# Interleaved row blocks in the last unit's gate product, one store for each of its row tiles, and pair 5's query sums and key copies at the end of the step

## Chip, cores and metric

The kernel runs on one core of a Trainium2 chip. The metric is the device time of one execution in microseconds; the time given for a kernel is the median of its runs. The engines are named as in the profile: PE is TensorE, ACT is ScalarE, DVE is VectorE, POOL is GpSimd, SP is SyncE.

## The reference

Attention with pooled queries, and after it a feed-forward part with a gate:

```python
q_pool = q.reshape(B, H, S // 2, 2, D).mean(axis=3)      # B=8, H=8, S=1152, D=64
scores = (1 / sqrt(D)) * q_pool @ k.transpose(0, 1, 3, 2)
attn = softmax(scores)                                   # over 1152 keys
x = (attn @ v).transpose(0, 2, 1, 3).reshape(B * 576, 512)
out = ((x @ w1) * (x @ w2) @ w3) @ w_out                 # d_ff = 1024, out 4608 x 512 float32
```

## The kernel before

**Pairs and steps.** Two heads make a pair; there are 32 pairs, with 576 pooled queries and 9 blocks of 128 keys each. The scores of all pairs, laid end to end, are cut into 324 chunks of 512 columns. The main loop (`for it in range(NIT)`, L598) has 108 steps. A step issues three chunks: `scores` (L301) makes the matmuls into one of three PSUM buffers named `psc`, which are taken in turn, and `expo` (L319) takes the exponential on ScalarE into a ring in SBUF. After the chunks a step issues attention matmuls (`attend`, L330, whose counts are written out by hand in `PVS`), and between them one or two groups from a queue (`group`, L551): a group of kind "F" has a PSUM buffer `ff` of its own, a group of kind "X" takes the next `psc` buffer. A group issues its matmuls and then its eviction. Each engine works through its instructions in the order in which the program issues them.

**What the groups are.** First the weights: w3 is transposed (`w3_group`, L402, evicted to `w3T` at L411) and multiplied by w_out (`T_group`, L414, evicted to `T16` at L422), so that w3 @ w_out becomes one matrix. Then the feed-forward units: 512 rows of x each, nine in all (`ffn_groups`, L425). A unit has 8 pairs of groups `pa` and `pb` (x @ w1 and x @ w2, transposed: features on partitions, rows in columns), whose product is written to `gT` at L446, and then four row blocks of 128 rows (`rows`, L449), which multiply `gT` by `T16`, evict to a row tile `osb` (L461 on ScalarE, L464 on VectorE) and store it (L473). The first seven units are issued between the attention's groups; what remains runs behind the attention, with `tail` set.

**Preparing a pair.** Pairs 1 to 7 are prepared on VectorE and TensorE. `prep_stage` (L162) issues two VectorE instructions: the sums of neighbouring queries (L121, from the staged queries `qst`) and a copy of the keys into another order (L165, from `kst`). One step later `prep_groups` (L270) is put at the head of the queue: TensorE transposes sums and keys (L278, L169), and VectorE copies them to `qT` and `kT` (L284 to L292). From pair 8 on, `prep_dma` does this with GpSimd and DMA transposes instead. The loop calls `prep_stage` in two places:

```python
        if 5 <= staged < NPE and it >= first_it(staged) - 3:     # L615: ahead of the step's groups
            prep_stage(staged)
            staged += 1
...
        if staged < 5 and it >= first_it(staged) - 2:            # L648: behind the step's groups
            prep_stage(staged)
            staged += 1
            more_loads(staged)
```

`first_it(5)` is 16, so pair 5 is prepared in step 13, whose chunks are 39 to 41. That step's groups are a w3 transposition (kind F) and a T group (kind X). Loads of queries, keys and values are issued on POOL's queue, in a written order.

**Stores.** Row p * 9 + c of a batch's output belongs to query block c, so a row tile of 128 rows covers two query blocks of 64 rows, the lower and the upper half of its partitions. Each half is stored by a DMA of its own, 64 rows with a step of 9 rows in the output. The very last row block (`final`) is computed in pieces of 256, 128 and 128 columns, each evicted and stored by itself; there the upper half's store is issued on ScalarE's queue, all others on SyncE's.

Of the kernel before, what the change touches and what calls it, by code (L numbers as in the profile page):

```python
# [14 lines left out]
SQ = 576  # L15
NJ = 9
# [7 lines left out]
def kernel(  # L24
# [11 lines left out]
    nc = tc.nc  # L36
    B, H, S, D = q.shape
    dm = H * D
# [6 lines left out]
    NPE = 8  # L45
# [13 lines left out]
    T16 = const.tile([128, NF, dm], FP16)  # L59
# [39 lines left out]
    def load(P):  # L99
        if P < NP:  # L100
            load_k(P)
            load_q(P)
            load_v(P)
# [32 lines left out]
    def prep_dma(P):  # L136

        pool_q(P, 2)
        for p in (P, P + 1):
            new_kq(p)  # L140
            nc.gpsimd.tensor_copy(  # L141
                out=new_kc(p).rearrange("p j u d -> p u j d").bitcast(mybir.dt.int32),
                in_=kst.pop(p).bitcast(mybir.dt.int32))
        for p in (P, P + 1):
            nc.sync.dma_start_transpose(
                out=kT[p], in_=kcs[p].rearrange("p j u d -> p (j u d)"))
            if p == P:
                nc.sync.dma_start_transpose(
                    out=qTs[P // 2], in_=qps[P // 2].rearrange("p c u d -> p (c u d)"))
# [12 lines left out]
    def prep_stage(P):  # L162

        pool_q(P)
        nc.vector.tensor_copy(out=new_kc(P).rearrange("p j u d -> p u j d"), in_=kst.pop(P))  # L165
# [135 lines left out]
    def scores(c):  # L301
        t = psum.tile([128, 2, CH], FP32, tag="psc", bufs=3, name="psc")
        psc[c] = t
        if 3 <= c < 10:
            nc.tensor.matmul(t[:, 0], ones[:, 0:128], ones, start=True, stop=True)
        g = c * CH
        while g < (c + 1) * CH:
            J = g // SQ
            P, j = divmod(J, NJ)
            f0 = g - J * SQ  # L310
            ln = min(SQ - f0, (c + 1) * CH - g)
            o = g - c * CH
            for u in range(2):
                s = slice(64 * u, 64 * u + 64)
                nc.tensor.matmul(t[:, u, o:o + ln].rearrange("p (c f) -> p c f", f=64), kT[P][s, j, :],  # L315
                                 qT[P][s, f0 // 64:(f0 + ln) // 64], start=True, stop=True)
            g += ln

    def expo(c):  # L319
        r = (c * CH) % RING  # L320
        g = (c - RING // CH + 1) * CH
        if g > 0:
            Pg, Jg = divmod((g - 1) // SQ, NJ)
            assert nb >= 90 * Pg + 45 + 5 * Jg + 5
        nc.scalar.activation(out=er[:, :, r:r + CH], in_=psc.pop(c), func=AF.Exp,  # L325
                             bias=0.0, scale=SCALE)
# [69 lines left out]
    tail = False  # L396
# [28 lines left out]
    def ffn_groups(t):  # L425
        t0 = 512 * t
        gT = ffp.tile([128, NF, 512], FP16, tag="g", name="gT")
        asb = {}

        def half(ft, name):  # L430
            w = w1sb if name == "pa" else w2sb

            def mm(p, mc):
                nc.tensor.matmul(p, w[:, mc, ft * 128:ft * 128 + 128],  # L434
                                 xT[:, mc, t0:t0 + 512],
                                 start=(mc == 0), stop=(mc == NC - 1))

            def end(p):
                if name == "pa":
                    asb[ft] = ffp.tile([128, 512], FP32, tag="asb", name="asb")  # L440
                    if tail:
                        nc.scalar.copy(out=asb[ft], in_=p)  # L442
                    else:
                        nc.vector.tensor_copy(out=asb[ft], in_=p)  # L444
                else:
                    nc.vector.tensor_mul(out=gT[:, ft, :], in0=p, in1=asb.pop(ft))  # L446
            return name, FP32, NC, mm, end

        def rows(i, o, n):  # L449

            def mm(p, ft):
                nc.tensor.matmul(p[:, 0:n], gT[:, ft, 128 * i:128 * i + 128],  # L452
                                 T16[:, ft, o:o + n],
                                 start=(ft == 0), stop=(ft == NF - 1))

            def end(p):
                if o == 0:
                    osbs[i] = ffp.tile([128, dm], FP32, tag="osb", bufs=6, name="osb")
                osb = osbs[i][:, o:o + n]
                if tail and not (final and o):  # L460
                    nc.scalar.activation(out=osb, in_=p[:, 0:n], func=AF.Copy, bias=0.0,  # L461
                                         scale=1.0 / (SCL * SCL))
                else:
                    nc.vector.tensor_scalar_mul(out=osb, in0=p[:, 0:n],  # L464
                                                scalar1=1.0 / (SCL * SCL))
                if not final and o + n < dm:
                    return
                cs = slice(o, o + n) if final else slice(0, dm)
                for z in range(2):
                    b, f = divmod(t0 + 128 * i + 64 * z, SQ)  # L470
                    dst = out[b * SQ:(b + 1) * SQ, :].rearrange("(p c) m -> c p m", c=NJ)
                    eng = nc.scalar if final and z else nc.sync
                    eng.dma_start(out=dst[f // 64][:, cs], in_=osbs[i][64 * z:64 * z + 64, cs])  # L473
            final = t == n_units - 1 and i == 3
            return "pp", FP32, NF, mm, end

        osbs = {}
        for ft in range(NF):
            yield half(ft, "pa")
            yield half(ft, "pb")  # L480
        for i in range(4):
            last = t == n_units - 1 and i == 3
            widths = (256, 128, 128) if last else (512,) if tail else (256, 256)
            for x, n in enumerate(widths):
                yield rows(i, sum(widths[0:x]), n)


    NCHUNK = NP * PAIR // CH
# [6 lines left out]
        out=ident, in_=ident, compare_op=ALU.not_equal, fill=1.0,  # L495
# [16 lines left out]
    loaded, staged, prepped, copied = 8, 1, 1, 1  # L512
# [24 lines left out]
    n_units = NT // 512  # L537
# [37 lines left out]
    def first_it(P):  # L575
        return P * PAIR // (CH * BURST)
# [21 lines left out]
    for it in range(NIT):  # L598
        at = it * BURST * CH / PAIR
        while early and it >= early[0][0]:  # L600
            queue.append(early.pop(0)[1])
        while next_unit < EARLY:
            last_b = (512 * (next_unit + 1) - 1) // SQ
            if it < 3 or reached[it - 2] < 360 * (last_b + 1):
                break
            gens.append(ffn_groups(next_unit))
            next_unit += 1
        for w in range(BURST):
            if it == 0 and w == 2:
                some()  # L610
            if it == 1 and w == 1:
                rest()
            scores(BURST * it + w)
            expo(BURST * it + w)
        if 5 <= staged < NPE and it >= first_it(staged) - 3:  # L615
            prep_stage(staged)
            staged += 1
        while 8 <= loaded < NPE + 2 and at >= loaded - 3.4:
            load(loaded)
            loaded += 1  # L620
        urgent = False
        if prepped < NPE:
            if it >= first_it(prepped) - (1 if prepped < 5 else 2):
                queue[0:0] = prep_groups(prepped)
                prepped += 1
                urgent = True
        elif prepped < NP and at >= prepped - 1.95:
            prep_dma(prepped)
            if loaded < NP:
                settled(prepped)  # L630
                load_two(loaded)
                loaded += 2
            prepped += 2
        if NPE <= copied < NP and at >= copied - 1.1:
            copy_v(copied)
            copied += 1
        n = PVS[it]
        left = 45 - nb % 45
        brief = bool(queue) and queue[0][2] == 1
        a = left if left < n else 8 if brief and it > 8 and 8 < n < 40 and 8 < left < 45 else 0  # L640
        assert nb + n <= NPV and ready(nb + n - 1, BURST * it)
        pv(a)
        if head():
            group("F")
        if head() and (n < 40 or urgent or it < 17):
            group("X")
        pv(n - a)
        if staged < 5 and it >= first_it(staged) - 2:  # L648
            prep_stage(staged)
            staged += 1  # L650
            more_loads(staged)
        if copied < NPE and at >= copied + (0.25 if copied < 5 else 0):
            copy_v(copied)
            copied += 1
        reached.append(nb)
# [6 lines left out]
    tail = True  # L662
# [36 lines left out]
```

The softmax here doesn't subtract the row's maximum and nothing guards it: scores larger than these inputs give would overflow.

## Time and profile before

| | |
|---|---|
| median of 13 runs | 419.07 us (418.31 to 421.5) |
| the profiled execution | 418.76 us, of which its span 417.0 us |
| mean granted TensorE clock | 0.997 |
| ScalarE's exponentials (L325) | 324, 307.3 us busy, 1028 ns each |
| attention matmuls (L340) | 2880, 110.3 us busy |
| gate products (L446) | 72, 49.8 us busy, 691 ns each |
| output stores (L473) | 76 DMAs |

The span runs from the first to the last instruction of the program. A line of a timeline gives the start, the length, the engine, the source line, the operation with its tiles and shapes, the number of instructions merged, and in brackets how long the engine had been idle before and what ended that. An engine's name with a q behind it (SPq, ACTq) is its instruction queue issuing a DMA. A line of waits gives the engine and line that waited, what it waited for, the total, the number of times and the longest. "To landing" is the time from a DMA's issue until its completion was signalled.

### The profile page before, as it was taken

What the parts mean: (1) busy time and instruction counts of PE and PEld (TensorE: products, weight loads), DVE (VectorE), ACT (ScalarE), POOL (GpSimd) and SP (SyncE); (2) the same over time, 40 slices, a digit from 0 to 9 for tenths busy, and PEclk for the clock granted to TensorE, in tenths of its full rate; (3) what the DMA queues carried; (4) which work ended last, traced back from release to release, by engine and by line L of the source; (5) the groups of instructions that cost most, each with busy time, mean ns of one, the idle gap of its engine ahead of it and who ended that gap; (6) DMA issues with size and microseconds to landing.
All of it is one profiled execution on the core that took longest, in us unless ns stands there. A gap on an engine that the chain in (4) does not pass through costs nothing.

```text
span 417.0 us, 12724 instructions
## 1 busy us (share of the span) xinstructions
PE 406.1 (97%) x5497; PEld 270.4 (65%) x5497; DVE 199.7 (48%) x408; ACT 326.0 (78%) x356; POOL 121.2 (29%) x161
## 2 busy tenths in 40 slices
PE   8999899999999999999999999999999999999994
PEld 5677777766775677666866686668656866544442
DVE  3546666455445643544455644554555345613130
ACT  5999899889888899988888898898888999032321
POOL 7533431343435262534524305252430000000000
PEclk9999999999999999999999999999999999999998
DMA  8999999799999999999999959997993351050404
GB/s 202 202 204 189 184 205 191 117 158 157 146 168 204 158 187 191 171 166 146 189 216 139 182 92 200 146 176 137 193 165 63 53 80 31 2 116 2 101 0 103
DMA packets 96489, 59.76 MB, mean 143 GB/s; under 512 B 65584, under 2 KB 86704, under 8 KB 96432
## 3 DMA queue, kind: packets, MB, share of 16 engines
q0 software_dynamic: 26928, 32.97, 50.5%
q1 hardware_dynamic: 69264, 25.84, 37.3%
q8 instruction: 43, 0.70, 0.7%
q10 hardware_dynamic: 240, 0.13, 0.1%
q14 instruction: 14, 0.11, 0.1%
HBM read 67.11 MB, written 9.44 MB: 184 GB/s over the span
## 4 chain that ended last, share of the span: by engine, by line
PE 85%; DMA 10%; ACT 2%; POOL 1%; issue 1%; DVE 1%; ACTq 0%; POOLq 0%
PE po L340 19%; PE psc L315 17%; PE pa L434 16%; PE pp L452 16%; PE pb L434 15%; DMA qst<-in_q_dram 4%; DMA kst<-in_k_dram 3%; DMA w3h<-in_moe_w_dram 2%; ACT er L325 2%; PE pT L418 2%; DMA er<-in_k_dram 1%; POOL kst L88 0%; POOL w3h L379 0%; PE t L169 0%; POOL vst L95 0%
## 5 line engine op out<-in xcount | busy, mean ns | idle before, releaser
L325 ACT ACTIVATE er<-psc 128x1024 f16<-128x1024 f32 x324 | 307.3, 1028 | 41.4 <-PE psc L315 41.2
L340 PEld LDWEIGHTS <-er 128*128 128x128 f16 x2880 | 103.3, 97 | 22.0 <-issue 5.9
L340 PE MATMUL po<-vt,er 128*128 128x65 f16 x2880 | 110.3, 193 | 0.0
L315 PE MATMUL psc<-qT,kT 64*128 64x512 f16 (+7 forms) x1152 | 95.0, 285 | 3.5 <-ACT er L325 2.0
L446 DVE TENSOR_TENSOR gT<-pb,asb 128x512 f16<-128x512 f32 x72 | 49.8, 691 | 56.0 <-PE pb L434 55.2
L434 PE MATMUL pa<-xT,w1sb 128*128 128x512 f16 x288 | 74.2, 380 | 0.0
L434 PE MATMUL pb<-xT,w2sb 128*128 128x512 f16 x288 | 74.1, 380 | 0.0
L452 PE MATMUL pp<-T,gT 128*128 128x256 f16 (+2 forms) x496 | 67.9, 290 | 0.0
L315 PEld LDWEIGHTS <-kT 64*128 64x128 f16 x1152 | 45.5, 94 | 28.5 <-issue 9.8
L452 PEld LDWEIGHTS <-gT 128*128 128x128 f16 x496 | 45.9, 98 | 18.4 <-issue 3.7
L444 DVE COPY asb<-pa 128x512 f32<-128x512 f32 x56 | 38.7, 691 | 38.2 <-PE pa L434 37.1
L434 PEld LDWEIGHTS <-w2sb 128*128 128x128 f16 x288 | 26.4, 98 | 32.7 <-issue 3.9
L434 PEld LDWEIGHTS <-w1sb 128*128 128x128 f16 x288 | 25.1, 98 | 30.1 <-issue 6.2
L121 POOL TENSOR_TENSOR qp<-qst 128x1152 f16<-128x1152 f16 x12 | 28.3, 2355 | 55.9 <-issue 27.6
L464 DVE TENSOR_SCALAR osb<-pp 128x256 f32<-128x256 f32 (+1 forms) x50 | 21.0, 419 | 38.6 <-PE pp L452 38.6
L353 DVE RECIPROCAL rz<-po 128x5 f32<-128x5 f32 x64 | 12.4, 193 | 47.9 <-PE po L340 47.5
L141 POOL COPY kc<-kst 128x576 int32<-128x576 int32 x24 | 16.5, 688 | 57.0 <-issue 41.7
L357 DVE TENSOR_TENSOR xn<-po,rz 128x320 f16<-128x320 f32 x64 | 31.5, 492 | 2.2
L95 POOL DMA_DIRECT2D vst<-in_v_dram x32 | 23.4, 742 | 11.9 <-DVE T L422 4.3
L461 ACT ACTIVATE osb<-pp 128x512 f32<-128x512 f32 (+1 forms) x12 | 7.0, 579 | 24.0 <-PE pp L452 20.4
L88 POOL DMA_DIRECT2D kst<-in_k_dram x31 | 22.6, 745 | 9.3 <-DVE kT L285 2.3
L442 ACT COPY asb<-pa 128x512 f32<-128x512 f32 x16 | 9.4, 586 | 16.5 <-PE pa L434 16.5
(49 smaller groups left out, 151.9 us busy)
## 6 DMA issues: line engine op xcount, KB each, us to landing
vst<-in_v_dram POOLq DMA_DIRECT2D x32, 288.0 KB, 10.4
out_dram<-osb SPq DMA_DIRECT2D x70, 128.0 KB, 2.5
qst<-in_q_dram POOLq DMA_DIRECT2D x31, 288.0 KB, 7.2
kst<-in_k_dram POOLq DMA_DIRECT2D x31, 288.0 KB, 12.8
w3h<-in_moe_w_dram POOLq DMA_DIRECT2D x3, 512.0 KB, 14.3
xT<-in_moe_w_out_dram POOLq DMA_DIRECT2D x4, 256.0 KB, 10.1
w1sb<-in_moe_w_dram POOLq DMA_DIRECT2D x2, 512.0 KB, 16.8
w2sb<-in_moe_w_dram POOLq DMA_DIRECT2D x2, 512.0 KB, 16.9
```

Of the source, the lines that this page charges most:

```text
L88: nc.gpsimd.dma_start(out=kst[P].rearrange("p u j d -> p u (j d)"), in_=k[b, h0:h0 + 2].rearrange("u (p j) d -> p u (j d)", j=NJ))
L95: nc.gpsimd.dma_start(out=vst[P].rearrange("p u j d -> p u (j d)"), in_=v[b, h0:h0 + 2].rearrange("u (p j) d -> p u (j d)", j=NJ))
L121: eng.tensor_tensor(out=qps[pp][r].rearrange("p c u d -> p u c d"), in0=src[:, :, :, 0, :], in1=src[:, :, :, 1, :], op=ALU.add)
L315: nc.tensor.matmul(t[:, u, o:o + ln].rearrange("p (c f) -> p c f", f=64), kT[P][s, j, :], qT[P][s, f0 // 64:(f0 + ln) // 64], start=True, ...
L325: nc.scalar.activation(out=er[:, :, r:r + CH], in_=psc.pop(c), func=AF.Exp, bias=0.0, scale=SCALE)
L340: nc.tensor.matmul(po[P, u][:, VW * x:VW * x + D + 1], er[:, u, r:r + 128], vts[P % 4][:, u, j, 0:D + 1], start=(m == 0), stop=(m == 44), ...
L357: nc.vector.tensor_tensor(out=xn[:, P % 2, :, u, :], in0=acc[:, :, 0:D], in1=rz.to_broadcast([128, 5, D]), op=ALU.mult)
L434: nc.tensor.matmul(p, w[:, mc, ft * 128:ft * 128 + 128], xT[:, mc, t0:t0 + 512], start=(mc == 0), stop=(mc == NC - 1))
L444: nc.vector.tensor_copy(out=asb[ft], in_=p)
L446: nc.vector.tensor_mul(out=gT[:, ft, :], in0=p, in1=asb.pop(ft))
L452: nc.tensor.matmul(p[:, 0:n], gT[:, ft, 128 * i:128 * i + 128], T16[:, ft, o:o + n], start=(ft == 0), stop=(ft == NF - 1))
L464: nc.vector.tensor_scalar_mul(out=osb, in0=p[:, 0:n], scalar1=1.0 / (SCL * SCL))
```

## The change

Two parts, independent of each other.

In the last unit (`t == n_units - 1`) the gate product is written with the two halves of each 128-row block interleaved: column r of the lower half and column r of the upper half stand side by side. A row tile's partitions then hold rows of the two query blocks in turn, and in the output such a pair of rows is 1024 contiguous elements. One DMA on SyncE's queue stores the row tile. The last row block is computed in two pieces of 256 columns, the first evicted by ScalarE and the second by VectorE, each stored by one DMA on SyncE's queue. For all other units evictions and stores stay as they are.

Pair 5's `prep_stage` moves from the first of the two places in the loop to the second, in the same step 13; pairs 6 and 7 stay in the first. `more_loads`, which is called behind it there, issues loads only when its argument is 2, 3 or 4.

```diff
                 else:
-                    nc.vector.tensor_mul(out=gT[:, ft, :], in0=p, in1=asb.pop(ft))
+                    o, a = gT[:, ft, :], asb.pop(ft)
+                    if t == n_units - 1:
+                        o = o.rearrange("f (i r z) -> f i z r", i=4, z=2)
+                        p = p.rearrange("f (i z r) -> f i z r", i=4, z=2)
+                        a = a.rearrange("f (i z r) -> f i z r", i=4, z=2)
+                    nc.vector.tensor_mul(out=o, in0=p, in1=a)
...
-        def rows(i, o, n):
+        def rows(i, s, n):
...
-                cs = slice(o, o + n) if final else slice(0, dm)
+                cs = slice(n * s, n * s + n) if final else slice(0, dm)
+                if t == n_units - 1:
+                    b, f = divmod(t0 + 128 * i, SQ)
+                    dst = out[b * SQ:(b + 1) * SQ, :].rearrange("(p c) m -> p c m", c=NJ)
+                    nc.sync.dma_start(out=dst[:, f // 64:f // 64 + 2, cs], in_=osbs[i][:, cs])
+                    return
                 for z in range(2):
                     b, f = divmod(t0 + 128 * i + 64 * z, SQ)
                     dst = out[b * SQ:(b + 1) * SQ, :].rearrange("(p c) m -> c p m", c=NJ)
-                    eng = nc.scalar if final and z else nc.sync
-                    eng.dma_start(out=dst[f // 64][:, cs], in_=osbs[i][64 * z:64 * z + 64, cs])
+                    nc.sync.dma_start(out=dst[f // 64], in_=osbs[i][64 * z:64 * z + 64])
...
-            last = t == n_units - 1 and i == 3
-            widths = (256, 128, 128) if last else (512,) if tail else (256, 256)
-            for x, n in enumerate(widths):
-                yield rows(i, sum(widths[0:x]), n)
+            if tail and not (t == n_units - 1 and i == 3):
+                yield rows(i, 0, 512)
+            else:
+                yield rows(i, 0, 256)
+                yield rows(i, 1, 256)
...
-        if 5 <= staged < NPE and it >= first_it(staged) - 3:
+        if 6 <= staged < NPE and it >= first_it(staged) - 3:
...
-        if staged < 5 and it >= first_it(staged) - 2:
+        if staged < 6 and it >= first_it(staged) - (2 if staged < 5 else 3):
             prep_stage(staged)
             staged += 1
             more_loads(staged)
```

More of the change, by code (lines that the diff above doesn't have):

```diff
@@ L445, in end @@
                 else:
-                    nc.vector.tensor_mul(out=gT[:, ft, :], in0=p, in1=asb.pop(ft))
+                    o, a = gT[:, ft, :], asb.pop(ft)
[4 more added lines that the diff above has]
+                    nc.vector.tensor_mul(out=o, in0=p, in1=a)
             return name, FP32, NC, mm, end
-        def rows(i, o, n):
+        def rows(i, s, n):
             def mm(p, ft):
                 nc.tensor.matmul(p[:, 0:n], gT[:, ft, 128 * i:128 * i + 128],
-                                 T16[:, ft, o:o + n],
+                                 T16[:, ft, n * s:n * s + n],
                                  start=(ft == 0), stop=(ft == NF - 1))
             def end(p):
-                if o == 0:
+                if s == 0:
                     osbs[i] = ffp.tile([128, dm], FP32, tag="osb", bufs=6, name="osb")
-                osb = osbs[i][:, o:o + n]
-                if tail and not (final and o):
+                osb = osbs[i][:, n * s:n * s + n]
+                if tail and not (final and s):
                     nc.scalar.activation(out=osb, in_=p[:, 0:n], func=AF.Copy, bias=0.0,
@@ L465, in end @@
                                                 scalar1=1.0 / (SCL * SCL))
-                if not final and o + n < dm:
+                if not final and n * (s + 1) < dm:
                     return
-                cs = slice(o, o + n) if final else slice(0, dm)
+                cs = slice(n * s, n * s + n) if final else slice(0, dm)
[4 more added lines that the diff above has]
+                    return
                 for z in range(2):
```

## The prediction

> **What bounds the kernel now.** I read the page's engine rows first, then the waits of TensorE, then the timelines round the one wait that the moved step could touch, and last the tail after the final matmul.
>
> ```profile
> PE 406.1 (97%) x5497; PEld 270.4 (65%) x5497; DVE 199.7 (48%) x408; ACT 326.0 (78%) x356; POOL 121.2 (29%) x161
> PE 85%; DMA 10%; ACT 2%; POOL 1%; issue 1%; DVE 1%; ACTq 0%; POOLq 0%
> ```
>
> TensorE (PE) is busy 97% of the 417.0 us, and the chain that ended last is 85% TensorE. So time can be won only where TensorE stands still, or before its first and after its last matmul. Its waits (engine, line, releaser: total us, times, longest):
>
> ```profile
> PE psc L315 <- ACT er L325: 2.0, 7, 0.5
> PE psc L315 <- DVE T L422: 0.9, 1, 0.9
> ```
>
> One wait is on VectorE (DVE), a single time, 0.9 us. From 73 us on, TensorE has no recorded wait above 0.06 us: what it is late at 73 us, it is late at the end. VectorE and TensorE round that wait (start, length):
>
> ```profile
> 46.26 0.76 DVE L121 TENSOR_TENSOR qp<-qst 64x1152 f16<-64x1152 f16 x1 [1.68 <-DMA qst<-in_q_dram]
> 47.05 0.46 DVE L165 COPY kc<-kst 128x1152 f16<-128x1152 f16 x1
> 47.43 0.68 DVE L411 COPY w3T<-w3t 128x1024 f16<-128x1024 f16 x1
> 48.03 0.42 DVE L422 CAST T<-pT 128x256 f16<-128x256 f32 x1
> ```
>
> ```profile
> 45.36 1.04 PE L418 MATMUL pT<-xT,w3T 128*128 128x256 f16 x8
> 46.23 0.83 PE L340 MATMUL po<-vt,er 128*128 128x65 f16 x22
> 46.99 0.61 PE L315 MATMUL psc<-qT,kT 64*128 64x384 f16 x8
> 48.50 0.39 PE L315 MATMUL psc<-qT,kT 64*128 64x512 f16 x2 [0.89 <-DVE T L422]
> ```
>
> This is pair 5's preparation (step 13). VectorE stood 1.68 us before its query sums because pair 5's queries landed only at 46.24. Two evictions, ready in PSUM since 45.52 (L406) and 46.40 (L418), queued behind it and ran at 47.43 and 48.03. Scores take one of three `psc` buffers in turn; chunk 44 needed the one the late T eviction held, so TensorE stood 0.89 us. ScalarE (ACT) felt it one chunk later, idle 0.75 us:
>
> ```profile
> 51.09 1.02 ACT L325 ACTIVATE er<-psc 128x1024 f16<-128x1024 f32 x1 [0.75 <-PE psc L315]
> ```
>
> The tail:
>
> ```profile
> 411.11 1.73 ACTq L473 DMA_DIRECT2D out_dram<-osb  x1
> ```
>
> ```profile
> 411.59 0.29 DVE L464 TENSOR_SCALAR osb<-pp 128x128 f32<-128x128 f32 x1 [0.15 <-PE pp L452]
> ```
>
> ```profile
> 413.59 0.81 ACTq L473 DMA_DIRECT2D out_dram<-osb  x1
> ```
>
> ```profile
> out_dram<-osb ACTq DMA_DIRECT2D x1, 32.0 KB, 2.1
> ```
>
> The last matmul ends at 411.57 and the last eviction at 411.89, but the last store is issued only at 413.59: ScalarE's queue has three stores, the first took 1.73 us to issue, the second started at 412.94. The last lands at 413.59 + 2.12 = 415.70. SyncE then runs through its closing waits to 416.15, and the closing barrier ends the span at 417.0.
>
> **What the Trainium skill says.** "VectorE: DVE Perf Modes", section "Why PSUM operands drop a tier": an fp32 operand in PSUM holds the operation at 1x. The gate product is already there (512 elements in 691 ns, 0.74 elements per ns, overhead included), so a spread output has no faster mode to lose. "DMA: Bandwidth & Descriptors", section "Issuing engines are not separate DMA queues": stores from two engines share the same 16 DMA engines and a second issuer saves only issue time; here ScalarE's issues took 0.55 to 1.73 us and SyncE's 0.47 to 0.60, so it did not even save that. Same page, "Why a DMA increments its semaphore by 16 and not by 1": a transfer uses the largest count up to 16 that divides the slowest dimension of both sides. The new store has 64 rows on one side and 128 partitions on the other, so 16; no run here shows this shape yet.
>
> **The change, part by part.**
>
> 1. *Gate products of the last unit* (8 of 72, L446): same 512 elements, only the fp16 output steps by two. No row shows a stepped output. Bounds: 0.69 us each (no change) to twice, 1.38; a gain is excluded, since the work is the same. VectorE is idle 1.03 us before each (0.69 in a period of 1.73 us), so even 1.38 is hidden, and the last product, begun at 404.72, is needed by the first row block's eighth matmul at about 404.61 + 7 x 0.216 = 406.1. I take 0; if the cover were gone, up to 0.1.
>
> 2. *Row tiles 0 to 2 of the last unit*: one 256 KB store for two of 128 KB. Before, the pair was issued within 1.11 us (406.995 to 408.10) and TensorE needs 1.73 us per tile. No effect on the end except for what is still moving when the last tile comes.
>
> 3. *Row tile 3*: 256 + 128 + 128 columns become 256 + 256. TensorE: the 16 matmuls of 128 columns start 0.056 us apart, 0.90 us; 8 of 256 at 0.109 are 0.87 us: -0.02. Its last eviction is 128x256 on VectorE, 0.42 us (the other L464 rows) instead of 0.29. So: matmuls end 411.55, VectorE ends 411.99, SyncE issues at 412.01 (it issued 0.03 us after the eviction for tile 0). SyncE is free: tile 2's single store goes out at 410.45, tile 3's first half, evicted at 411.08, at 411.11. The six stores of the last tile become two, all of ScalarE's disappear.
>
> Landing: a 128 KB store took 2.24 to 2.39 us from issue, so 414.25 to 414.40 if nothing is in front. In front are tile 2's 256 KB and tile 3's first 128 KB. The first tile's 256 KB moved from 408.17 to 409.35 (about 0.6 us per 128 KB, first byte 1.2 us after issue, 0.5 us from last byte to landing). So tile 2's data run 411.65 to 412.85, the first half's to 413.45, the last half's to 414.05, landing 414.55. I take 414.5, a gain of 1.2 us on 415.70. SyncE's closing waits are about 0.06 us each and six of them followed the last landing; with another store last in the round of eight semaphores, 0 to 6 follow: +0.1 on average. **Tail: 1.3 us**, bounds 0.9 (256 KB issue as slow as 0.6 us, more contention) and 1.7.
>
> 4. *Pair 5's preparation to the end of step 13.* It is two VectorE instructions and issues no DMA (the load list called after it has no entry for 6), so no queue of SyncE or POOL moves. It passes, on VectorE, the w3T copy and the T cast. POOL's later loads into the buffers that it frees go out at 58.79 and 61.61, over 10 us later.
> VectorE after: w3T copy at 45.55, T 46.42 to 46.85, query sums 46.87 to 47.62 (queries there since 46.24), key copies 47.65 to 48.11.
> TensorE after: chunk 44 follows chunk 43 at 47.60, 0.90 us earlier. Then 8 attention matmuls, then pair 5's query transposes at about 48.27 (before 49.17): they need the sums at 47.62, 0.65 us to spare; the key transposes at 48.6 need 48.11. Chunk 45 is done about 0.9 us earlier, and ScalarE starts it right behind chunk 44, at 49.31 + 0.90 = 50.22 instead of 51.09: 0.87 us. Chunk 46 needs chunk 44's buffer, free at 50.34, so TensorE gives back 0.3 us there (0.6 left); but it regains 0.14 at 54.00, where it waited for ScalarE's chunk 47, which now comes 0.87 us earlier. About 0.75 us on both engines. The remaining waits between the two (0.32, 0.19, 0.18, 0.26 us, up to 73 us) move with them.
> What could be late next is what DMA fixes in time: pair 8's transposed queries landed at 87.10 and are first used at 88.81; 1.7 us of spare against 0.75. **Step 13: 0.75 us**, bounds 0.6 and 0.89. A loss is excluded while the sums meet their 0.65 us of spare.
>
> *Sum:* the profiled execution took 418.76 us (span 417.0 and 1.76 round it). 418.76 - 1.3 - 0.75 = 416.7. The median of the 13 runs is 0.31 above the profiled one: 419.07 - 2.05 = **417.0**. Its own range, from the bounds: 419.07 - 2.59 to - 1.5, 416.5 to 417.6.
>
> **Rivals.**
> A. *Only the tail gains.* The 0.75 us at step 13 turns into new waits on ScalarE (for: between 55 and 73 us TensorE waits for it four times, and it is then busy without a gap for nine chunks; against: it starts 0.87 us earlier too). 419.07 - 1.3 = 417.8.
> B. *Only step 13 gains.* The last store now waits for its data behind 384 KB on one queue and lands at about 415.5 (for: DMA share is 0.82 at 411.5 to 413.1; against: 128 KB a piece at 0.6 us). 419.07 - 0.75 - 0.2 = 418.1.
> C. *Neither is seen*: 419.
> D. *Slower: the new store's shape runs on few DMA engines.* If two dimensions of the destination are ordered so that only two engines serve it, 128 KB at 1/8 of 16 engines takes 0.6 x 8 = 4.8 us, 4.2 more, and with 2.05 won: 421.2. It decides from 0.6 x 16/n - 0.6 > 2.05, n under 4. Against: rows come first on both sides (64 and 128), and the old stores with 64 rows landed in 2.2 to 2.4 us.
>
> **How the numbers follow.** Forecast 0.66, A 0.12, B 0.12, C 0.04, D 0.06. A range of 416.2 to 418.2 holds the forecast, A and B nearly whole, with 0.3 us for the medians' own scatter: about 0.85. Faster by over 0.2% (0.84 us, below 418.23; about what a measurement of this kernel can tell from no change): forecast, A and most of B, 0.87. Same: the rest of B and C, 0.07. Slower: D, 0.06.
>
> **What would show it.** Right: no TensorE wait on L422 in step 13; query sums after the T cast with no wait for queries; ScalarE's chunk 45 directly behind 44; TensorE's last matmul about 0.75 us earlier; no store on ScalarE's queue; last store issued within 0.1 us of the last eviction, landing in about 2.5 us; gate products at 0.69 us. Wrong: a new TensorE wait on the query sums or at pair 8's first scores, a landing above 3.5 us for the 256-column store, or gate products above 1.7 us.

## The result and the profile after

The changed kernel takes **416.53 us** in the median of 11 runs (416.21 to 417.69), against 419.15 us for the kernel before, measured again in 48 runs. The ratio is 0.9937, with a 95% interval of 0.9923 to 0.9951. The forecast was 417.0 us. The profiled execution took 416.55 us, with a span of 414.8. (Of the experiments below, e3's profiled execution ran at about half speed throughout; its trace is not used.)

The first part of the page again, and the chain that ended last:

```profile
PE 406.3 (98%) x5489; PEld 270.4 (65%) x5489; DVE 198.3 (48%) x407; ACT 325.9 (79%) x356; POOL 120.9 (29%) x161
PE 89%; DMA 5%; ACT 4%; issue 1%; DVE 0%; ACTq 0%; POOL 0%
```

TensorE did the same work in a shorter span. Its waits on other engines, the longest row (engine, line, releaser: total us, times, longest):

```profile
PE psc L315 <- ACT er L325: 2.5, 8, 0.5
```

The row with the T cast of L422 is gone; the one on ScalarE has grown from 2.0 us in 7 waits to 2.5 in 8. VectorE in step 13 (start, length):

```profile
45.87 0.69 DVE L411 COPY w3T<-w3t 128x1024 f16<-128x1024 f16 x1 [0.98 <-PE w3t L406]
46.74 0.42 DVE L422 CAST T<-pT 128x256 f16<-128x256 f32 x1 [0.18 <-PE pT L418]
47.20 0.76 DVE L121 TENSOR_TENSOR qp<-qst 64x1152 f16<-64x1152 f16 x1
```

Both evictions now wait for TensorE, not the other way round, and the query sums start with no wait. TensorE:

```profile
47.31 0.83 PE L315 MATMUL psc<-qT,kT 64*128 64x384 f16 x10
48.07 0.42 PE L340 MATMUL po<-vt,er 128*128 128x65 f16 x8
...
49.87 0.39 PE L315 MATMUL psc<-qT,kT 64*128 64x512 f16 x2
50.71 0.61 PE L315 MATMUL psc<-qT,kT 64*128 64x64 f16 x8 [0.45 <-ACT er L325]
```

Chunks 42 to 44 run as one row of ten matmuls; before, eight ran and two stood 0.89 us. The wait that comes instead is at 50.71, where chunk 46 needs the buffer that ScalarE is still reading. The tail (the last eviction, the last store's issue, and what the stores took to land):

```profile
411.16 0.42 DVE L469 TENSOR_SCALAR osb<-pp 128x256 f32<-128x256 f32 x1 [6.13 <-PE pp L457]
```

```profile
411.61 0.54 SPq L477 DMA_DIRECT2D out_dram<-osb  x1
```

```profile
out_dram<-osb SPq DMA_DIRECT2D x3, 256.0 KB, 2.4
out_dram<-osb SPq DMA_DIRECT2D x2, 128.0 KB, 2.1
```

The last store is issued 0.03 us after the last eviction, and nothing stands in front of it. It lands at 413.67.

**Where the 2.2 us of the two spans went.** The steps ahead of step 13 are the same program in both kernels but don't run alike in two executions: chunk 39's exponential, the first of step 13, started at 44.18 us before and at 44.49 after. So I count from there.

| stretch | before | after | difference |
|---|---|---|---|
| start to chunk 39 | 44.18 | 44.49 | +0.31 |
| chunk 39 to chunk 69 (step 23) | 32.24 | 31.51 | -0.73 |
| chunk 69 to the end of the last matmul | 335.14 | 335.12 | -0.02 |
| last matmul to the last landing | 4.14 | 2.55 | -1.59 |
| last landing to the end of the span | 1.28 | 1.11 | -0.17 |
| span | 416.98 | 414.78 | -2.20 |

### The profile page after: what moved, and what is told of

Its sections match the earlier page's. It is cut to its first block, busy times and chain, and to the rows that moved or that the text cites. A ratio compares the mean times of both kernels' runs of the same rounds, so it can differ in the third digit from the quotient of the medians.

```text
span 414.8 us, 12696 instructions
## 1 busy us (share of the span) xinstructions
PE 406.3 (98%) x5489; PEld 270.4 (65%) x5489; DVE 198.3 (48%) x407; ACT 325.9 (79%) x356; POOL 120.9 (29%) x161
## 4 chain that ended last, share of the span: by engine, by line
PE 89%; DMA 5%; ACT 4%; issue 1%; DVE 0%; ACTq 0%; POOL 0%
PE po L340 20%; PE psc L315 19%; PE pa L434 16%; PE pp L457 16%; PE pb L434 15%; ACT er L325 4%; DMA qst<-in_q_dram 3%; PE pT L418 3%; DMA vst<-in_v_dram 1%; DMA er<-in_k_dram 1%; PE w3t L406 0%; PE t L169 0%; DVE kc L165 0%; DVE osb L469 0%; ACTq L325 0%
## 5 line engine op out<-in xcount | busy, mean ns | idle before, releaser
L457 PE MATMUL pp<-T,gT 128*128 128x256 f16 (+1 forms) x488 | 67.9, 292 | 0.0
L469 DVE TENSOR_SCALAR osb<-pp 128x256 f32<-128x256 f32 x49 | 20.8, 424 | 38.7 <-PE pp L457 38.6
```

The source lines that it names most:

```text
L469: nc.vector.tensor_scalar_mul(out=osb, in0=p[:, 0:n], scalar1=1.0 / (SCL * SCL))
```

## Experiments

The theory: two gains that have nothing to do with each other, one at step 13, where evictions stood behind a wait for pair 5's queries, one in the tail, where stores stood behind one another's issues. The main rivals: only one of the two is real; at step 13 it is the place and not the wait that matters; in the tail it is ScalarE's queue, or the shape of the transfers, and not the number of issues. All measures in one table; the last three columns come from each kernel's trace. The ratio is the recorded estimate against runs of the kernel before made beside the same experiment, and not the quotient of the two medians. Where its interval reaches 1 (e3, e4, e6), the times can't tell the kernel from the one before, and what is said of it rests on its trace.

| kernel | median us | ratio to before (95%) | chunk 39 to last matmul | last matmul to last issue | last matmul to last landing |
|---|---|---|---|---|---|
| before | 419.15 | | 367.38 | 2.03 | 4.14 |
| changed | 416.53 | 0.9937 (0.9923-0.9951) | 366.63 | 0.49 | 2.55 |
| e1 move only | 418.44 | 0.9978 (0.9964-0.9991) | 366.64 | 2.20 | 4.16 |
| e2 tail only | 417.69 | 0.9977 (0.9958-0.9997) | 366.90 | 0.49 | 2.55 |
| e3, e12 all on SyncE | 419.15 (e3) | 0.9990 (0.9968-1.0012) | 366.82 (e12) | 3.24 (e12) | 5.14 (e12) |
| e4 two pieces | 417.93 | 0.9991 (0.9970-1.0013) | 366.64 | 1.40 | 3.69 |
| e5 three pieces, paired | 416.71 | 0.9953 (0.9938-0.9968) | 366.67 | 0.84 | 2.76 |
| e6 early load | 418.69 | 0.9989 (0.9976-1.0003) | 368.37 | 1.99 | 3.84 |
| e7 paired, in halves | 418.52 | 0.9985 (0.9972-0.9998) | 366.65 | 2.05 | 4.11 |
| e8 two evictions | 417.06 | 0.9949 (0.9937-0.9960) | 366.68 | 0.66 | 2.72 |
| e9 early, thin | 416.74 | 0.9943 (0.9923-0.9964) | 366.66 | 0.39 | 2.45 |
| e10 all stepped | 416.98 | 0.9952 (0.9933-0.9971) | 366.94 | 0.49 | 2.55 |
| e11 all at the end | 417.93 | 0.9976 (0.9956-0.9996) | 367.19 | 0.49 | 2.55 |

### One part alone: e1 and e2

e1 is the kernel before with this edit alone; e2 is the changed kernel with it taken back:

```diff
-        if 5 <= staged < NPE and it >= first_it(staged) - 3:
+        if 6 <= staged < NPE and it >= first_it(staged) - 3:
...
-        if staged < 5 and it >= first_it(staged) - 2:
+        if staged < 6 and it >= first_it(staged) - (2 if staged < 5 else 3):
```

Expected of e1: 

> The kernel before with only pair 5's preparation moved to the end of step 13; the last unit as before. Theory (two independent gains, 0.75 us at step 13 and the rest in the tail): TensorE has no wait on the T cast in step 13, chunk 45's exponential starts 0.87 us earlier relative to the steps ahead of it, everything from step 17 on 0.74 us earlier, and from the last matmul to the last landing still 4.1 us; 419.15 - 0.75 = 418.4 us. Rival (the move gives nothing by itself, new waits on ScalarE take its place and the whole gain is in the tail): 419.15 us, chunks of step 17 and later where they were.

Expected of e2: 

> The changed kernel with pair 5's preparation put back ahead of step 13's groups. Theory: the 0.89 us wait of TensorE on the T cast is back; from the last matmul to the last landing 2.5 us instead of 4.1, and three closing waits behind the landing instead of six; 419.15 - 1.6 - 0.2 = 417.35 us. Rival (the tail's stores only look shorter because they start earlier, or wait for their data): 418.3 us or above, last landing more than 3 us behind the last matmul.

e1 came out at 418.44 us, 0.77 under the 419.21 us of the kernel before in the same runs, and its trace has 366.64 us from chunk 39 to the last matmul (the changed kernel 366.63) with the old tail of 4.16. So the move gives a gain by itself, and the rival of a tail-only gain falls; by the times alone the size is loose, its interval runs from 0.4 to 1.5 us. e2 came out at 417.69 us, 0.3 above the expectation, with two of its 14 runs above 421; its interval ends just short of the expected gain (ratio 0.9958, against 0.9957 for 417.35 us). Its tail is the changed kernel's to the hundredth.

In e2 the wait on the T cast is back, but smaller than in the kernel before:

```profile
45.93 0.76 DVE L121 TENSOR_TENSOR qp<-qst 64x1152 f16<-64x1152 f16 x1 [1.23 <-DMA qst<-in_q_dram]
```

```profile
PE psc L315 <- DVE T L422: 0.4, 1, 0.4
```

Here pair 5's queries landed 1.60 us after chunk 39's start (45.90 and 44.30), in the kernel before 2.06 (46.24 and 44.18). The queries were 0.46 us earlier relative to the step, the wait was 0.46 shorter, and up to the last matmul this execution lost 0.27 us against the changed kernel instead of 0.75. The stall's size is a race between a DMA and the steps, and differs from execution to execution: in the eleven traces with this load order the queries landed 1.48 to 3.43 us after chunk 39's start.

### Is it the place or the wait? e6 and e11

e6 leaves the preparation in its old place and brings the data earlier:

```diff
             load_w3(4, 2)
-            load_w3(6, 2)
             load_k(5)
             load_q(5)
+            load_w3(6, 2)
             load_v(4)
```

Expected of e6: 

> The kernel before, preparation in its old place, tail as before; only pair 5's keys and queries are loaded ahead of w3's last quarter instead of behind it. Theory (it was the wait for pair 5's queries, standing ahead of two evictions, that stalled TensorE): queries land near 42.5 us, query sums start without a wait at about 44.6, the T cast ends near 46.95, ahead of chunk 44's turn at 47.6; no TensorE wait there and the same 0.75 us: 418.4 us. Rival (the place matters: 1.2 us of preparation ahead of the evictions is enough to stall TensorE): wait on the T cast still above 0.3 us, 418.8 to 419.15 us.

VectorE in e6's step 13:

```profile
45.50 0.75 DVE L121 TENSOR_TENSOR qp<-qst 64x1152 f16<-64x1152 f16 x1
46.29 0.46 DVE L165 COPY kc<-kst 128x1152 f16<-128x1152 f16 x1
46.66 0.69 DVE L411 COPY w3T<-w3t 128x1024 f16<-128x1024 f16 x1
47.32 0.42 DVE L422 CAST T<-pT 128x256 f16<-128x256 f32 x1
```

The queries landed at 44.47, no wait, and TensorE has no wait on L422. From chunk 39 to chunk 69 e6 takes 31.51 us, the same as the changed kernel. So 1.2 us of preparation ahead of the evictions is harmless there; the wait for the queries was the cause. The landing time I expected (42.5) was 2 us too early. The median, 418.69 us, is 0.3 above the expectation and 0.1 below the rival's range, so it is the trace that decides. The traced execution was e6's slowest (420.35 us): TensorE stood 1.57 us at 155.7 us in a row-block group with no releaser that the profile shows, which makes up most of what the 368.37 in the table is above the others' 366.6. What that was stays open; it isn't in the other traces.

e11 turns the question round and moves pairs 6 and 7 to the end of their steps too:

```diff
-        if 6 <= staged < NPE and it >= first_it(staged) - 3:
+        if 8 <= staged < NPE and it >= first_it(staged) - 3:
...
-        if staged < 6 and it >= first_it(staged) - (2 if staged < 5 else 3):
+        if staged < 8 and it >= first_it(staged) - (2 if staged < 5 else 3):
```

Expected of e11: 

> The changed kernel with pairs 6 and 7 also prepared at the end of their steps (17 and 20). Theory (it was pair 5's late queries, not the place): pairs 6's and 7's queries are there long before, nothing waited in front of their evictions, so nothing is gained: 416.5 us. Rival (the place itself costs: two evictions held up by 1.2 us): 0.2 us or more faster, and fewer TensorE waits between 57 and 70 us.

Neither was right: it is slower, 417.93 us, and 0.56 us longer from chunk 39 to the last matmul. For pair 6 (VectorE, then TensorE):

```profile
60.32 0.49 DVE L357 TENSOR_TENSOR xn<-po,rz 128x320 f16<-128x320 f32 x1
60.73 0.74 DVE L121 TENSOR_TENSOR qp<-qst 64x1152 f16<-64x1152 f16 x1
```

```profile
60.24 0.57 PE L315 MATMUL psc<-qT,kT 64*128 64x448 f16 x6
61.52 0.43 PE L278 MATMUL t<-ident,qp 64*128 64x64 f16 x9 [0.71 <-DVE qp L121]
```

At the end of step 17 the sums stand behind a normalization, so they come too late for the transposes of step 18, where TensorE waits 0.71 us; with the changed kernel those transposes start without a wait, and a 0.32 us wait on ScalarE follows them. The end of the step isn't the better place in general: it has a limit of its own, the next step's transposes. Pair 6's wait costs 0.41 of the 0.56 us. The other 0.15 has nothing to do with e11's edit: pair 5's queries landed 3.43 us after chunk 39's start, VectorE waited for them, and pair 5's transposes stood 0.27 us (at 48.83). The changed kernel's place is thus not safe either. In e8's trace, where pair 5's queries landed 3.34 us after chunk 39's start, the sums waited for them even there, and TensorE for the sums (0.18 us).

### What the tail is made of: e3, e12, e4, e5 and e7

All have the move. e3 (and e12, the same kernel once more for its profile) keeps the old tail but issues every store on SyncE's queue; e4 keeps halves and both queues, but cuts the last tile in two pieces:

```diff
-                    eng = nc.scalar if final and z else nc.sync
-                    eng.dma_start(out=dst[f // 64][:, cs], in_=osbs[i][64 * z:64 * z + 64, cs])
+                    nc.sync.dma_start(out=dst[f // 64][:, cs], in_=osbs[i][64 * z:64 * z + 64, cs])
```

```diff
-            widths = (256, 128, 128) if last else (512,) if tail else (256, 256)
+            widths = (256, 256) if last else (512,) if tail else (256, 256)
```

Expected of e3: 

> Preparation moved as in the change; tail as before (halves apart, three pieces of the last tile, two stores each), but all stores on SyncE's queue. Theory (the tail is a row of issues: each store costs 0.5 to 0.6 us on the queue that issues it): the last tile's six stores follow one another on SyncE, the last is issued about 1.0 us later than ScalarE's last one was, landing 5 us behind the last matmul; 419.15 - 0.75 + 0.95 = 419.35 us. Rival (ScalarE's queue alone was slow, with its 1.73 us first issue, and the number of stores doesn't matter): 417.8 us or below.

Expected of e12: 

> The kernel of e3_all_sync once more for a profile at full clock: all stores of the unchanged tail on SyncE's queue, preparation moved. Theory: six stores of the last tile issued back to back at 0.5 to 0.65 us each, the last issued about 3.5 us and landed about 5.4 us behind the last matmul; 419.2 us.

Expected of e4: 

> Preparation moved as in the change; halves apart and the upper halves' stores on ScalarE's queue as before, but the last tile in two pieces of 256 columns instead of three. Theory (row of issues): ScalarE's first issue still takes about 1.7 us and its second, now the last, goes out right behind it, 0.65 us earlier than the third did; 419.15 - 0.75 - 0.6 = 417.8 us. Rival (the number of issues doesn't matter, the last store waits for its data): 418.4 us.

e3 gave 419.15 us: by the medians the whole gain of the move is spent again. In e12 SyncE issues one store right behind another from 410.66 on, and its last store goes out 3.24 us behind the last matmul and lands 5.14 us behind it, each about 0.3 us sooner than expected:

```profile
415.00 0.59 SPq L472 DMA_DIRECT2D out_dram<-osb  x1
```

(One run of e12 took 419.84 us.) So ScalarE's queue, slow as it was, took over work that SyncE alone needed longer for (3.24 us against 2.03); it isn't the cause by itself. In e4 ScalarE's first issue is again the long one:

```profile
411.88 1.73 ACTq L473 DMA_DIRECT2D out_dram<-osb  x1
```

Its second, now the last, follows at 413.70, 1.40 us behind the last matmul instead of 2.03, as the row of issues said, and lands 0.45 us sooner than before. The median, 417.93 us, is nearer to 417.8 than to the rival's 418.4, but with three of 12 runs above 420 its interval holds 418.4 and just misses 417.8; the trace decides.

e5 and e7 take the changed kernel's interleaved rows and give issues back. e5 has three pieces (256, 128, 128 columns) with one store each; e7 stores each row tile in two:

```diff
-                    nc.sync.dma_start(out=dst[:, f // 64:f // 64 + 2, cs], in_=osbs[i][:, cs])
+                    for z in range(2):
+                        nc.sync.dma_start(out=dst[32 * z:32 * z + 32, f // 64:f // 64 + 2, cs],
+                                          in_=osbs[i][64 * z:64 * z + 64, cs])
```

Expected of e5: 

> The changed kernel, but the last tile in three pieces of 256, 128 and 128 columns, one store each on SyncE's queue. Theory (row of issues): the last eviction is 0.13 us shorter, but its store queues behind the second piece's, issued about 0.25 us later than the changed kernel's last: 416.8 us. Rival (the last eviction and the size of the last transfer decide): 416.4 us.

Expected of e7: 

> The changed kernel with its interleaved rows, but each row tile of the last unit stored by two DMAs, partitions 0 to 63 and 64 to 127, all on SyncE's queue. Theory (what counts is that there are half as many issues): SyncE issues four stores for the last tile, each 0.5 to 0.6 us, the last about 1.2 us later than in the changed kernel: 417.75 us. Rival (what counts is that two rows lie side by side in the output, 4 KB in one piece): 416.6 us.

e5: 416.71 us; its last eviction is 0.13 us shorter, yet the store behind it is issued 0.84 us after the last matmul instead of 0.49, because the second piece's store is still being issued. e7: 418.52 us, with the last landing 4.11 us behind the last matmul, as in the kernel before, though each pair of rows still lies side by side in the output. Its last store took 2.06 us from issue to landing, the same as the changed kernel's; only the issue came later. So the number of issues decides, in both directions, and contiguous rows stored in halves gave nothing. e7's median is 0.8 us above its expectation; by its trace it should be about 1.6 us above the changed kernel, and it is 2.0.

### What is still to be had: e8, e9 and e10

e8 evicts the very last 256 columns on both engines at once:

```diff
-                if tail and not (final and s):
+                if final and s:
+                    nc.scalar.activation(out=osb[:, 0:128], in_=p[:, 0:128], func=AF.Copy, bias=0.0,
+                                         scale=1.0 / (SCL * SCL))
+                    nc.vector.tensor_scalar_mul(out=osb[:, 128:n], in0=p[:, 128:n],
+                                                scalar1=1.0 / (SCL * SCL))
+                elif tail:
```

Expected of e8: 

> The changed kernel; the very last 128x256 eviction is split, 128 columns on ScalarE and 128 on VectorE at the same time, one store behind both. Theory (behind the last matmul one eviction, one issue and one landing stand in a row): the last eviction takes 0.29 instead of 0.42 us, the last store is issued 0.1 us earlier, 416.4 us against 416.53 (too little for the times, read from the trace). Rival (the two engines hinder each other at the same PSUM bank, or the store waits for two engines): last store issued no earlier, 416.5 to 416.7 us.

```profile
411.29 0.28 ACT L466 ACTIVATE osb<-pp 128x128 f32<-128x128 f32 x1 [0.49 <-PE pp L457]
411.60 0.29 DVE L468 TENSOR_SCALAR osb<-pp 128x128 f32<-128x128 f32 x1 [6.44 <-ACT osb L466]
```

VectorE waited for ScalarE's semaphore: the two ran one after the other, 0.6 us instead of 0.42. The last store was issued 0.66 us behind the last matmul instead of 0.49, as the rival said, and the time was 417.06 us in 5 runs, its interval overlapping the changed kernel's. Whether it was the shared PSUM tile or the shared row tile that tied them was not tried.

e9 gets at the same 0.1 us by two PSUM tiles, and has e6's earlier load besides:

```diff
+            if t == n_units - 1 and i == 3:
+                yield rows(i, 0, 256)
+                yield rows(i, 256, 128)
+                yield rows(i, 384, 128)
```

The second call's piece goes to ScalarE and isn't stored; the third's goes to VectorE, and one store of 256 columns follows it.

Expected of e9: 

> The changed kernel with two more edits: pair 5's keys and queries loaded ahead of w3's last quarter, and the second half of the last tile computed in two pieces of 128 columns, the first evicted by ScalarE while TensorE makes the second, the second by VectorE, one store for both. Theory: the last eviction takes 0.29 instead of 0.42 us and stands alone, so the last store is issued 0.1 us earlier behind the last matmul; step 13 no longer depends on when pair 5's queries arrive, so no execution stalls there; 416.4 us in the median, at best 0.1 to 0.2 us below the changed kernel. Rival (the two evictions of one tile still run one after the other, and loads in the other order cost elsewhere): 416.6 us or above.

The last store is issued 0.39 us behind the last matmul instead of 0.49, and landed 2.45 instead of 2.55, as expected. The time, 416.74 us (416.21 to 417.79, 6 runs), can't be told from the changed kernel's 416.53.

e10 steps the gate product's output in all nine units (`if True:` for `if t == n_units - 1:`, and the other units' stores read `osbs[i][z::2]`).

Expected of e10: 

> The changed kernel with the interleaved gate product in all nine units, not only in the last; the stores of the other units read every second partition. Theory (a stepped output costs VectorE 0.036 us more per product, and VectorE has idle time everywhere): 64 more products at 0.727 us, 2.3 us more VectorE work, hidden: 416.5 us. Rival (between the attention's groups the evictions hold PSUM buffers, so longer ones stall TensorE): 417 us or above, with new TensorE waits on the gate product.

All 72 products take longer (duration in ns least/median/most, first and last start in us):

```profile
L451 DVE TENSOR_TENSOR gT<-pb,asb x72: 726/736/755, 80.6 to 404.7; 128x512 f16<-128x512 f32 x72
```

Chunk 39 to the last matmul is 0.31 us longer, with no new TensorE wait above 0.07 us, and the median is 416.98 us: hidden for the most part. The intervals of the two kernels overlap; the loss is seen in the trace only.

## Why the prediction was right

The sum had two terms, 0.75 us at step 13 and 1.3 us in the tail; the trace has 0.73 and 1.76. The time, 0.5 us under the forecast, lies inside the range, and by 0.03 us inside the likeliest case's own range. The tail's 1.76 us lies outside the bounds that I gave it (0.9 to 1.7), and part of step 13's agreement is luck (5). Point by point:

1. *Gate products.* Taken at no change, bounded by 0.69 and 1.38 us. They take 0.727 us in the last unit, 5% more, hidden there as argued. The reason given, that an fp32 operand in PSUM leaves no faster mode to lose ("VectorE: DVE Perf Modes", "Why PSUM operands drop a tier"), fits a small change, but doesn't make it zero.

2. *Last matmul to last issue.* Predicted 0.46 us (411.55 to 412.01), measured 0.49. ScalarE's stores are gone and nothing queues on SyncE. Right, and e5, e7, e4 and e12 show that it is this row of issues that sets the tail. One remark was wrong: that the second issuer "did not even save" issue time. It saved 1.2 us (e12).

3. *Landing: the mis-sized term.* I put the last store behind 384 KB of data at 0.6 us per 128 KB and took 2.5 us from issue to landing. It took 2.06; the 256 KB stores took 2.40. The 0.6 us came from stores of 64 neighbouring partitions in the kernel before, and the new stores of 128 partitions move their data twice as fast. The DMA rows of the two kernels show it; 40 slices each, first the kernel before from 388 to 394 us, then the changed kernel from 405 to 417 us:

```profile
GB/s 205 232 205 205 69 0 0 109 259 218 177 137 260 205 191 164 28 0 14 205 218 205 191 205 232 205 205 69 0 0 109 259 218 150 150 232 205 218 178 28
```

```profile
GB/s 0 0 0 55 0 0 0 0 0 177 396 301 0 0 0 362 369 144 27 0 55 403 369 335 150 0 311 127 0 0 0 0 0 0 0 0 0 0 0 0
```

About 200 GB/s while the halves are stored, 300 to 400 in the full slices of the whole tiles. That made the difference between 1.2 and 1.59 us. Rival D, few DMA engines for the new shape, was wrong by the same rows, and rival B's wait for data didn't come about.

4. *Closing waits.* Taken as +0.1 us, with 0 to 6 of them behind the last landing; three were, and the stretch shrank by 0.17 us.

5. *Step 13.* ScalarE's chunk 45 started 0.87 us earlier relative to chunk 39 (6.04 us after it instead of 6.91), as worked out, and from step 17 on the gain is 0.74. In between it isn't what I said. At chunk 48 it was 0.43, because TensorE gave back more at chunk 46: a wait of 0.45 us by the record where I had 0.3. Against that, the old wait at 54.00 was worth more than the 0.14 that I counted. The three single sums were each off by 0.15 to 0.3 us, and the errors cancelled; that the sum came out was luck. One reason is to be seen in the timelines: a wait is counted from the modelled end of the matmul in front, and counted from start to start each of the three costs more. From the start of chunk 42 to the start of the attention matmuls behind chunk 44 the kernel before took 1.83 us and the changed one 0.76, a difference of 1.07 for a wait of 0.89. The same count gives 0.61 for the 0.45 at chunk 46 (49.87 to 51.25, before 50.60 to 51.37) and 0.32 for the 0.14 at 54.00 (before 53.46 to 54.54, now 53.35 to 54.11), and 1.07 - 0.61 + 0.32 = 0.78. The last matmul, which was to end about 0.75 us earlier, ended 0.45 earlier (411.12 after 411.57), because the steps ahead of step 13 ran 0.31 us later.

6. *A loss excluded at step 13.* That held in the profiled execution of the changed kernel (its sums ended 0.46 us ahead of their transposes), but "0.65 us to spare" was read from one arrival of the queries. e8 and e11 show TensorE waiting for the sums of pair 5 with the new order too, by 0.18 and 0.27 us, where they came late.

## What to carry to other kernels

Where an instruction on an in-order engine waits for a load, look at what stands behind it: here two evictions that had been ready since 45.52 and 46.40 us held a PSUM buffer, and 0.89 us of TensorE went with it. The cure is in the order or in the load, and each has a limit that the trace shows (the next consumer; the arrival). At the end of a kernel, count issues: with 0.5 to 0.6 us for each store on a queue, one store for a whole tile beat both two queues and finer pieces. And where executions drift against one another ahead of the edit, compare from the last event that both programs share; 0.3 us of drift would have hidden nearly half of what the move gave.

## What the runs showed that was not expected

*A store from 64 neighbouring partitions moves at half the rate.* The Trainium skill has it on "SBUF — State Buffer", section "Door 1: The DMA port swizzle": partitions 0 to 63 reach only half of the SBUF's ports, and 64 to 127 the other half. I had not used it. e10 stored the same 64 rows of 2 KB from every second partition, and its row for 388 to 394 us reads:

```profile
GB/s 328 396 123 0 0 0 0 287 396 191 0 164 382 314 14 0 0 0 96 382 341 55 14 341 396 123 0 0 0 0 287 396 191 0 177 382 301 14 0 0
...
out_dram<-osb SPq DMA_DIRECT2D x6, 128.0 KB, 2.0
```

Up to 396 GB/s instead of about 200, and a median of 2.0 us to landing instead of the 2.3 of the changed kernel's halves in the same stretch. That it isn't the rows lying side by side in the output shows in e7, which has such rows but 64 neighbouring partitions; its row from 405 to 417 us stays at about 200 GB/s:

```profile
GB/s 0 0 55 0 0 0 0 0 184 184 205 205 96 41 198 184 232 184 62 82 218 184 219 171 202 17 181 38 150 68 137 82 0 0 0 0 0 0 0 0
```

Both agree with the page.

*The interleaved output costs VectorE 0.036 us per 512 elements* (0.727 to 0.691) in the last unit's gate product. The output is stepped by two, and the product is also written as eight runs of 64 columns instead of one of 512; which of the two costs it was not tried.

*ScalarE's first store in the program took 1.70 to 1.73 us to issue* in the kernel before, e1, e4 and e6, its later ones 0.55 to 0.82. Why was not tried.
